# Interleaved rising and falling loads of batch 1, and one angle operation moved, in a fused Fourier mixing and SwiGLU kernel

## The chip, the cores and the metric

The kernel runs on one core of a Trainium2 chip. The metric is the time of one execution in device microseconds (us); smaller is better. The kernel before takes 603.95 us, the median of three runs (603.82 to 604.01). The profile shows one further execution, which took 604.29 us, of which 602.4 us are the span from its first to its last instruction.

The engines are TensorE (PE in the profile, its weight loads PEld), VectorE (DVE), ScalarE (ACT), GpSimd (POOL) and SyncE (SP), which here only issues DMAs (SPq). Each works through a queue of its own in order, and waits on semaphores for the others.

## The reference

```python
def _attn_ref(x):                       # x: (8, 3008, 256)
    X = np.fft.fft(x, axis=1)
    X = np.fft.fft(X, axis=2)
    return X.real
def _moe_ref(x, w_gate, w_val, w_out):  # 24064 tokens, 256 -> 1536 -> 256
    g = x @ w_gate
    silu = g * (1.0 / (1.0 + np.exp(-g)))
    val = x @ w_val
    return silu * val @ w_out
```

Eight batches of 3008 rows and 256 columns are Fourier transformed along both axes; the real part is fed, row by row, to a SwiGLU block with a hidden width of 1536.

## The kernel before, in words

**What it computes.** The column transform is folded into the weights: `Wp`, `Wq` and `Wm` are the gate and value weights multiplied by cosine and sine tables (`half_w`, L458, and `weight_op`, L1794). The row transform of a batch is done by folding its rows by symmetry into few sums, which are multiplied by cosine and sine tables (`Tab`) on TensorE. The results are put by VectorE into the tiles `Pt` (cosine part) and `Qt` (sine part) of 512 columns each (L636 in the start, L1773 later). A unit is one tile and one of the 12 blocks of 128 hidden rows. Part a (L1426) multiplies `Pt` and `Qt` with the weights and gives the values of the rows k; part b (L1482) adds the mirrored sine part and gives those of the rows M - k. VectorE, ScalarE and GpSimd form the products: `hp` (L1550 on VectorE, L1556 on GpSimd) for the rows k and `hm` (L1547 on GpSimd, two blocks at a time) for the mirrored ones. What `hm` reads, `sv`, is written by VectorE (L1539) and ScalarE (L1523) and has two buffers. The first tiles are done whole (L1353): `hp` at L1374 and `hm` at L1395, both on VectorE. TensorE then multiplies with `Wo` (L1598), ScalarE evicts (L1604), SyncE stores (L1610).

**The start.** Batch 0 is loaded, folded and transformed by code in a written order (L251 to L680), all engines at once. The part that the change touches stands from L559 on. GpSimd forms the first rows' coefficients (`heads`, L446), copies a column to `EOA` (L564), and later fills `kfO` with an iota (L674), multiplies it by four columns into `rrO`, rounded to whole turns (`turns`, L352, four operations of 376 columns), and subtracts what will be `BBa` (L678 to L680). VectorE forms the first transform's P puts (L636), waits for ScalarE's copy `od` (L631), forms the Q puts, and casts one half of `Wp` (L468). The angles (`angles`, L356) take the fraction of a turn, `kfO` times a column less the rounded product, one operation for each of two columns and each of two chunks `ch`; magnitude, cosine and sine follow (L362, L368, L365) and fill the table for odd rows, which batch 0's second transform needs (L1756, at 37 us). `kfO` and `rrO` lie in the half of the buffer `XA` that the falling rows of A use; the other half holds the second part of the raw weights.

**The planner.** All later work is added to a list (`S.add`) with an engine, an estimated cost, what it reads and writes, and a due time: TensorE's clock at that point, plus a shift by kind (`SHIFT`) and by tile (`BIAS`). `S.run` (L1174) plays this list with the estimated costs and writes each engine's queue in the order that results. It starts each engine at a given time (L1996). A DMA has two costs, `us` for SyncE's issue and `ring` for the transfer, and no more than eight are under way; in the program itself the DMAs take eight semaphores in turn, so an issue waits until the DMA eight places back has landed. So changed estimates alter no operation, but can change the order on any engine.

**The loads around the change.** Batch 1 is loaded in two parts, while the first tiles are computed: C, 60 rows of partitions (L152), then A, 128 partitions (L146). A part has rising rows, loaded by many small DMAs (C: 15 of 4 partitions, L158; A: 16 of 8 partitions, L148), and falling rows, loaded by few large ones (C: 8, L167, since batch 1 has to lie in partitions 64 to 123 for one half and 0 to 59 for the other; A: 4 of 128 partitions, L150). C of batch 1 also has a load of row 0 (L160) and a copy of its rising rows within the chip (L171), which waits for all 15 rises. All are issued by SyncE: the rises of a part first, then its falls. `run_loads` (L1659) adds four loads for each unit to the planner. Ahead of them SyncE writes zeros to `XC` (L660), and GpSimd's queue loads the second part of the raw weights (L387) and `Wo` (L1970, landed at 36.42 us).

GpSimd folds each part (L173): `cross` (L180 and L181), `even` (L184), `odd` (L187), `ab` (L190), `ce` (L193, L194) and `bb` (L202 to L204). The folds of C and A of batch 1 stand in GpSimd's queue among the `hm` products, in the order that the planner gave.

Of the kernel before, what the change touches and what calls it, by code (L numbers as in the profile page):

```python
# [13 lines left out]
I32 = mybir.dt.int32  # L14
# [17 lines left out]
def kernel(  # L32
# [8 lines left out]
    nc = tc.nc  # L41
# [4 lines left out]
    G = M // 8  # L46
# [19 lines left out]
    NCR = GH - P  # L66
# [64 lines left out]
    LA, NA = 8, P // 8  # L131
# [8 lines left out]
    def down_set(b, a, j, L, n):  # L140

        return rows_at(b, R * (a + 1) - 2 * j, [[2 * L * D, n], [-2 * D, L], [1, 2 * D]])

    JA, JC = P - LA + 1, GH - LC + 1

    def load_a(b, q):  # L146
        X3 = XA.rearrange("p a q d -> p a (q d)")
        return ([lambda h=h: q.dma_start(out=X3[LA * h:LA * (h + 1), 0:4, :],  # L148
                                         in_=up_block(b, JA - LA * h, LA)) for h in range(NA)] +
                [lambda a=a: q.dma_start(out=X3[:, 4 + a, :], in_=down_set(b, a, JA, LA, NA)) for a in range(4)])  # L150

    def load_c(b, q):  # L152

        X3 = XC.rearrange("p a q d -> p a (q d)")
        p0 = 64 * (b % 2)
        pm = p0 + NCR
        r = slice(p0, p0 + NCR)
        ups = [lambda h=h: q.dma_start(out=X3[p0 + LC * h:p0 + LC * (h + 1), 0:4, :],  # L158
                                       in_=up_block(b, JC - LC * h, LC)) for h in range(NC_)]
        mid = [lambda: q.dma_start(out=XC[pm:pm + 1, 0:4, 1],  # L160
                                   in_=rows_at(b, 0, [[R * D, 1], [R * D, 4], [1, D]]))]
        if b != 1:
            return ups + [lambda a=a: q.dma_start(out=X3[r, 4 + a, :], in_=down_set(b, a, JC, LC, NC_))
                          for a in range(4)] + mid

        def down(a, k):
            q.dma_start(out=XC[0:NCR, 4 + a, 0] if k else XC[r, 4 + a, 0],  # L167
                        in_=rows_at(b, R * (a + 1) - 2 * JC + k, [[2 * LC * D, NC_], [-2 * D, LC], [1, D]]))

        downs = [[lambda a=a, k=k: down(a, k) for a in range(4)] for k in range(2)]  # L170
        return ups + downs[0] + mid + [lambda: q.dma_start(out=XC[0:NCR, 0:4, 1], in_=XC[r, 0:4, 0])] + downs[1]  # L171

    def fold_steps(eng, X, CE, BB, q, r):  # L173
        tt = eng.tensor_tensor
# [74 lines left out]
    q = nc.sync  # L249
# [103 lines left out]
        for i in range(2):  # L353
            pts(t1[:, i, :], kf, scalar1=mM[:, 2 * ch + i:2 * ch + i + 1], scalar2=1.0, op0=Alu.mult, op1=Alu.mult)

    def angles(rr, kf, ch, t1):  # L356
        for i in range(2):
            vstt(rr[:, i, :], kf, mM[:, 2 * ch + i:2 * ch + i + 1], t1[:, i, :],
                 op0=Alu.mult, op1=Alu.subtract)

# [85 lines left out]
    def heads(eng, ev, od, CE):  # L446

        eng.tensor_tensor(CE[:, :, 0, 0, -1:], ev, od, op=Alu.add)
        eng.tensor_tensor(CE[:, :, 0, 1, -1:], ev, od, op=Alu.subtract)
# [111 lines left out]
    ptt(hd, SA[:, 0, 0:2, :, 0:1], SA[:, 0, 2:4, :, 0:1], op=Alu.add)  # L561
    heads(nc.gpsimd, hd[:, 0], hd[:, 1], CEa)
    heads(nc.gpsimd, SC[:, 0, 0, :, 0:1], SC[:, 0, 1, :, 0:1], CEc)
    nc.gpsimd.tensor_copy(EOA[:, 0, :, :, P:P + 1], SA[:, 0, :, :, 0:1])  # L564
    ptile, qtile = {}, {}

# [45 lines left out]
    def transform(b, part, eos, given=None):  # L612
        n = NCE if part == 0 else G
        ev, ods = {}, {}
        for q, pool, nm in ((0, psO, "o"), (1, psG, "g")):
            if given:
                ps = {eo: given[eo][q] for eo in eos}
            else:
                ps = {eo: pool.tile([P, T], F32, name=nm) for eo in eos}
                for eo in eos:  # L620
                    mms = products(b, part, q, eo)
                    for i, (l, r_, cols) in enumerate(mms):
                        nc.tensor.matmul(ps[eo][:, cols], l, r_, start=(i == 0), stop=(i == len(mms) - 1),
                                         skip_group_check=True)
            if part == 0 and 1 in eos and not given:

                row0(b, q, ps[1])
            for eo in eos:
                if q == 0:
                    ods[eo] = odp.tile([P, NCE], F32, name="od")  # L630
                    nc.scalar.copy(ods[eo][:, 0:n], ps[eo][:, 0:n])  # L631
                else:
                    ev[eo] = ps[eo]

        def put(eo, dst, s0, w, minus):
            nc.vector.tensor_tensor(dst, ev[eo][:, s0:s0 + w], ods[eo][:, s0:s0 + w],  # L636
                                    op=Alu.subtract if minus else Alu.add)

        if part == 0:
            runs = [(0, GH, 1, 0), (GH, GH, 0, 1), (G, GH, GH + 1, 0), (G + GH, GH, GH + 1, 1)]  # L640
        else:
            runs = [(2 * G, G, 0, 0), (3 * G, G, 0, 1)]
        todo = []
        for eo in eos:
            for c0, n_, s0, minus in runs:
                for t, off, src, w in pieces(b * H + c0, n_):
                    todo.append((t, eo, off, s0 + src, w, minus))
        for t, eo, off, s0, w, minus in sorted(todo, key=lambda v: v[0:2]):
            put(eo, pq_tiles(t)[eo][:, off:off + w], s0, w, minus)
        if part == 0:  # L650
            for eo in eos:
                put(eo, last[eo][:, b:b + 1], 0, 1, 0)
# [8 lines left out]
                    in_=zeros[64 * hi + NCR:64 * hi + 64].unsqueeze(1).to_broadcast([64 - NCR, 16, D]))  # L661
    folded_c(0)
    transform(0, 0, (0,), acc)
    for k in range(2):
        half_w(0, k, psO, "o")
    folded_c(1)
# [4 lines left out]
    for k in range(2):  # L671
        half_w(1, k, psO, "o")
    double(1)
    nc.gpsimd.iota(kfO, pattern=[[4, G]], base=1, **iota)  # L674
    turns(rrO[:, 0].bitcast(I32), kfO, 0)
    turns(rrO[:, 1].bitcast(I32), kfO, 1)
    E_, O_ = EOA[:, 0].rearrange("p a q d -> p q a d"), EOA[:, 1].rearrange("p a q d -> p q a d")
    ptt(BBa[:, :, 0], E_[:, :, 0:4:3, 0:P], E_[:, :, 2:0:-1, 0:P], op=Alu.subtract)  # L678
# [980 lines left out]
    def run_loads(n):  # L1659
        for what, k, fn in loads[:n]:  # L1660
            up = k < (NA if what[0] == "A" else NC_)
            r, w, us, ring = [], [((what[0],), k)], 0.4 if up else 0.62, 0.57 if up or what[0] == "C" else 1.14
            if what == ("A", 1):
                r = [(("C",), NC_ + 9)]
                us, ring = 0.6, 0.6 if up else 0.9
            if what == ("C", 1):
                us, ring = (0.6, 0.6) if k < NC_ else (0.9, 0.9)
                if k == NC_ + 5:
                    r = [(("C",), j) for j in range(NC_)]
            S.add("SP", us, fn, r=r, w=w, after=[(("A",), "pre" if k > 15 else "preW")] if what == ("A", 1) else [],  # L1670
                  lat=2.5, ring=ring)
        del loads[:n]

# [160 lines left out]
    raO = SDf.rearrange("p a d -> p (a d)")[:, 0:4 * G].rearrange("p (c q n) -> p c q n", c=2, q=2)  # L1834

    def angle_op(ch):
        S.add("DVE", 1.1, lambda: angles(rrO[:, ch], kfO, ch, rrO[:, ch].bitcast(I32)),
              r=[(("A",), "pre")], w=[(("rr",), ch)])
        S.add("DVE", 0.7, lambda: magnitude(raO[:, ch], rrO[:, ch]), r=[(("rr",), ch), (("A",), "pre")],
              w=[(("ra",), ch), (("fold",), "F")])  # L1840
# [152 lines left out]
    part_b(prev)  # L1993
    owork = OWork(prev[0], ((psG, "g"), (psV, "v"), (psO, "o")))
    owork.run(len(owork.steps))
    S.run({'DVE': 1.2, 'ACT': 0.9, 'POOL': 3.5, 'PE': 0.0, 'SP': -2.0})  # L1996


# [28 lines left out]
```

## Time and profile before

| what | value |
|---|---|
| median of three runs | 603.95 us |
| the profiled execution | 604.29 us |
| its span | 602.4 us |
| 20 to 45 us: TensorE, VectorE, ScalarE, GpSimd busy | 24.01, 23.09, 23.33, 10.88 us |
| 45 to 64 us | 18.87, 17.74, 17.06, 14.33 us |
| 64 to 100 us | 35.24, 35.44, 32.43, 35.84 us |
| 100 to 150 us | 49.01, 47.72, 45.01, 49.69 us |
| share of the DMA engines busy, 0 to 30 us, in stretches of 10 us | 0.85, 0.99, 0.83 |
| granted clock of TensorE | 1.00 up to 580 us |

A row of a timeline reads: start in us, duration in us, engine, line, operation, tiles written and read, shape, number of like instructions merged; in brackets the idle time of the engine ahead of it and what ended it. A matmul's duration includes its passage through the array, so that rows overlap: the pace is read from one start to the next. The landing of a DMA is not in these rows; it is read from the updates of its semaphore in the trace.

### The profile page before, as it was taken

The numbers are of one execution on the slowest core, as the hardware profiler recorded it, in microseconds if no ns is written. First come the engines' busy times: TensorE is split into PE (matmuls) and PEld (weight loads), VectorE is DVE, ScalarE is ACT, GpSimd is POOL, SyncE is SP. The second block draws the span as 40 slices with busy tenths as digits, with TensorE's granted clock in tenths as the row PEclk, the third lists the DMA queues.
The fourth block names the chain that finished last, engine by engine and source line by source line (L and its number), as shares of the span: only waits on it lengthen the run. The fifth ranks groups of instructions, "written<-read, shape, count | busy, mean of one in ns | idle before, by whom it ended". The sixth has DMA issues, their size and how long they took to land.

```text
span 602.4 us, 12497 instructions
## 1 busy us (share of the span) xinstructions
PE 591.5 (98%) x3974; PEld 392.1 (65%) x4031; DVE 572.8 (95%) x1055; ACT 562.6 (93%) x1086; POOL 509.4 (85%) x460
## 2 busy tenths in 40 slices
PE   9999999999999999999999999999999999999997
PEld 6456666665666666666666666666666666666686
DVE  8989999999999999999999999999999999999993
ACT  8899997999998999999999999999999999999994
POOL 8736999999799999998999988888878467687772
PEclk9999999999999999999999999999999999999999
DMA  9847447254616324464145212036211212111112
GB/s 240 137 98 147 115 117 189 83 132 124 171 40 152 93 66 125 111 140 125 53 91 133 61 53 73 19 100 175 63 62 37 63 38 71 39 53 51 54 53 79
DMA packets 50554, 57.65 MB, mean 96 GB/s; under 512 B 7267, under 2 KB 37399, under 8 KB 50489
## 3 DMA queue, kind: packets, MB, share of 16 engines
q1 hardware_dynamic: 47529, 53.97, 33.4%
q0 software_dynamic: 2672, 2.36, 2.7%
q8 instruction: 31, 0.51, 0.4%
q10 hardware_dynamic: 288, 0.52, 0.3%
q14 instruction: 34, 0.28, 0.2%
HBM read 29.43 MB, written 24.65 MB: 90 GB/s over the span
## 4 chain that ended last, share of the span: by engine, by line
PE 81%; DMA 6%; DVE 4%; ACT 3%; POOL 2%; issue 2%; SPq 2%; POOLq 0%; ACTq 0%; DVEq 0%
PE o L1598 36%; PE g L1336 22%; PE v L1336 18%; PE g L1756 2%; DMA XC<-in_x_dram 2%; PE o L1756 2%; DMA XC<-Af 2%; DVE sv L1539 1%; DMA XA<-in_x_dram 1%; SPq L167 1%; DMA out_dram<-ev 1%; PE v L1598 1%; DVE hp L1550 1%; ACT sp L1448 1%; ACT v L1409 1%
## 5 line engine op out<-in xcount | busy, mean ns | idle before, releaser
L1547 POOL TENSOR_TENSOR hm<-sv 128x1024 bf16<-128x1024 f32 (+2 forms) x137 | 254.9, 1862 | 49.8 <-ACT sv L1523 23.0
L1539 DVE SCALAR_TENSOR_TENSOR sv<-es,v 128x512 f32<-128x512 f32 (+2 forms) x264 | 176.1, 672 | 5.9 <-PE v L1336 4.2
L1598 PE MATMUL o<-Wo,hm 128*128 128x256 bf16 (+1 forms) x1128 | 163.8, 272 | 0.4
L1550 DVE TENSOR_TENSOR hp<-sp,v 128x512 bf16<-128x512 f32 (+2 forms) x238 | 158.1, 672 | 4.4 <-PE v L1336 3.8
L1598 PE MATMUL o<-Wo,hp 128*128 128x256 bf16 (+1 forms) x1104 | 159.7, 272 | 0.7
L1598 PEld LDWEIGHTS <-hm 128*128 128x128 bf16 (+2 forms) x1140 | 111.7, 98 | 58.7 <-issue 2.1
L1598 PEld LDWEIGHTS <-hp 128*128 128x128 bf16 (+2 forms) x1140 | 111.9, 98 | 55.3 <-issue 2.0
L1523 ACT ACTIVATE sv<-g 128x512 f32<-128x512 f32 (+2 forms) x182 | 121.3, 682 | 5.5 <-PE g L1336 4.5
L1448 ACT ACTIVATE sp<-g 128x512 f32<-128x512 f32 (+2 forms) x182 | 113.4, 628 | 4.7 <-PE g L1336 1.9
L1409 ACT ACTIVATE v<-bc,w 128x512 f32<-128x512 bf16 (+2 forms) x146 | 105.9, 727 | 2.9 <-DVE hp L1550 1.6
L1336 PE MATMUL g<-Pt,Wp 128*128 128x512 bf16 (+2 forms) x282 | 105.6, 374 | 1.6 <-ACT sp L1520 0.7
L1336 PE MATMUL v<-Pt,Wp 128*128 128x512 bf16 (+2 forms) x287 | 105.2, 375 | 0.5
L1473 DVE SCALAR_TENSOR_TENSOR es<-bc,w,v 128x512 f32<-128x512 bf16 (+2 forms) x128 | 93.5, 734 | 2.8 <-PE v L1336 0.6
L1471 ACT ACTIVATE es<-v 128x512 f32<-128x512 f32 (+2 forms) x146 | 90.8, 625 | 4.5 <-PE v L1336 2.0
L1336 PE MATMUL g<-Qt,Wq 128*128 128x512 bf16 (+2 forms) x247 | 90.7, 374 | 0.3
L1336 PEld LDWEIGHTS <-Wp 128*128 128x128 bf16 x576 | 56.3, 98 | 26.9 <-issue 1.9
L1336 PE MATMUL g<-Qt,Wm 128*128 128x512 bf16 (+2 forms) x191 | 71.5, 376 | 0.4
L1452 DVE SCALAR_TENSOR_TENSOR sg<-bc,w,g 128x512 f32<-128x512 bf16 (+2 forms) x92 | 66.4, 724 | 1.4 <-PE g L1336 1.0
L1523 ACT ACTIVATE sv<-sg 128x512 f32<-128x512 f32 (+2 forms) x92 | 64.4, 704 | 1.0 <-DVE sg L1516 0.9
L1520 ACT ACTIVATE sp<-g 128x512 f32<-128x512 f32 (+2 forms) x92 | 57.3, 623 | 4.6 <-DVE sg L1516 4.4
L1516 DVE SCALAR_TENSOR_TENSOR sg<-sg,g 128x512 f32<-128x512 f32 (+2 forms) x92 | 60.9, 662 | 0.3 <-PE g L1336 0.2
L1336 PEld LDWEIGHTS <-Wq 128*128 128x128 bf16 x430 | 42.0, 98 | 28.1 <-issue 4.5
(196 smaller groups left out, 772.2 us busy)
## 6 DMA issues: line engine op xcount, KB each, us to landing
out_dram<-ev SPq DMA_DIRECT2D x96, 128.0 KB
XA<-in_x_dram SPq DMA_DIRECT2D x30, 256.0 KB
XA<-in_x_dram SPq DMA_DIRECT2D x112, 64.0 KB
XC<-in_x_dram SPq DMA_DIRECT2D x28, 120.0 KB
XC<-in_x_dram SPq DMA_DIRECT2D x105, 32.0 KB
bc<-br SPq DMA_DIRECT2D x19, 128.0 KB
St<-Fc SPq DMA_DIRECT2D x12, 128.5 KB
out_dram<-ev SPq DMA_DIRECT2D x12, 120.0 KB
```

The lines of the kernel that those rows point to most:

```text
L1336: nc.tensor.matmul(ps[:, :n], Wt[:, gv, fs], src[:, :n], start=start, stop=stop, skip_group_check=True)
L1409: nc.scalar.activation(T_[kv][:, :w], bc[t][:, :w], AF.Copy, scale=w0[:, 1, f:f + 1])
L1448: nc.scalar.activation(sp_to()[:, :w], T_[kg][:, :w], AF.Silu)
L1452: nc.vector.scalar_tensor_tensor(T_[keg][:, :w], bc[t][:, :w], w0[:, 0, f:f + 1], T_[kg][:, :w], op0=Alu.mult, op1=Alu.add)
L1471: nc.scalar.activation(T_[kes][:, :w], T_[kv][:, :w], AF.Copy, scale=2.0 if on_pool(u) > 1 else 1.0)
L1473: nc.vector.scalar_tensor_tensor(T_[kes][:, :w], bc[t][:, :w], w0[:, 1, f:f + 1], T_[kv][:, :w], op0=Alu.mult, op1=Alu.add)
L1516: nc.vector.scalar_tensor_tensor(T_[kgm][:, :w], T_[keg][:, :w], 2.0, T_[kg][:, :w], op0=Alu.mult, op1=Alu.subtract)
L1523: nc.scalar.activation(sv()[:, f % 2, w - 1::-1, 1], T_[kgm if by_dve else kg][:, :w], AF.Silu)
L1539: nc.vector.scalar_tensor_tensor(sv()[:, f % 2, w - 1::-1, 0], T_[kes][:, :w], 2.0, T_[kv][:, :w], op0=Alu.mult, op1=Alu.subtract)
L1547: nc.gpsimd.tensor_tensor(hts_(t)[1][:, f - 1:f + 1, :w], sv()[:, :, :w, 1], sv()[:, :, :w, 0], op=Alu.mult)
L1550: nc.vector.tensor_tensor(hts_(t)[0][:, f, :wp], T_[ksp][:, :wp], T_[kv][:, :wp], op=Alu.mult)
L1598: nc.tensor.matmul(st["ps"][:n, j, :], hts[t][minus][:, f, c:c + n], Wo[:, f, :], start=(f == 0), stop=(f == nF - 1))
```

## The change

Two things are moved, and the planner's estimates for batch 1's loads are set anew.

1. C of batch 1 is issued in the order `C1_ORDER`: u is a rise, d one of the first four falls, e one of the second four, m row 0, c the copy within the chip. A of batch 1 goes by `A1_ORDER`: four rises, one fall, four times.
2. The iota and the first two turns move on GpSimd from behind the start's last doubling to right behind the heads, ahead of the copy to `EOA`. The first of the four angle operations moves on VectorE out of the planner's list into the written start, between the P puts and the Q puts.
3. Estimates: a rise of C 0.35 and 0.45 us (issue and ring) instead of 0.6 and 0.6, a fall of C 0.85 and 0.75 instead of 0.9 and 0.9, a rise of A 0.35 and 0.5 instead of 0.6 and 0.6, a fall of A 0.65 and 0.9 instead of 0.6 and 0.9. A now follows C's last rise in the list instead of C's last fall, and SyncE starts at 1.0 instead of -2.0.

No operation is added or taken away: every engine has the same instructions in both programs, in another order. TensorE's order differs in its matmuls 129 to 249, 516 to 782 and 963 to 1047 of 4025, and in two swaps behind. GpSimd's queue has the first two rows of A's fold (L180, L181) and then: before, `hm`, `even`, `hm`, `odd`, `hm`, `ab`, `hm`; after, `even`, `odd`, `hm`, `hm`, `ab`. On VectorE one `hp` (L1550) and one `sv` (L1539) have changed places there. On SyncE eight C loads of the next batches stand ahead of the first stores.

```diff
+    C1_ORDER = "uuduuduuduuduumuueuueuece"
+    A1_ORDER = "uuuuduuuuduuuuduuuud"
+
     def load_a(b, q):
         X3 = XA.rearrange("p a q d -> p a (q d)")
-        return ([lambda h=h: q.dma_start(out=X3[LA * h:LA * (h + 1), 0:4, :],
+        res = ([lambda h=h: q.dma_start(out=X3[LA * h:LA * (h + 1), 0:4, :],
                                          in_=up_block(b, JA - LA * h, LA)) for h in range(NA)] +
                 [lambda a=a: q.dma_start(out=X3[:, 4 + a, :], in_=down_set(b, a, JA, LA, NA)) for a in range(4)])
+        return in_order(A1_ORDER, u=res[:NA], d=res[NA:]) if b == 1 else res
+
+    def in_order(order, **todo):
+        todo = {k: list(v) for k, v in todo.items()}
+        return [todo[k].pop(0) for k in order]
...
-        return ups + downs[0] + mid + [lambda: q.dma_start(out=XC[0:NCR, 0:4, 1], in_=XC[r, 0:4, 0])] + downs[1]
+        return in_order(C1_ORDER, u=ups, d=downs[0], e=downs[1], m=mid,
+                        c=[lambda: q.dma_start(out=XC[0:NCR, 0:4, 1], in_=XC[r, 0:4, 0])])
...
-    def angles(rr, kf, ch, t1):
-        for i in range(2):
+    def angles(rr, kf, ch, t1, only=(0, 1)):
+        for i in only:
...
     heads(nc.gpsimd, SC[:, 0, 0, :, 0:1], SC[:, 0, 1, :, 0:1], CEc)
+    nc.gpsimd.iota(kfO, pattern=[[4, G]], base=1, **iota)
+    turns(rrO[:, 0].bitcast(I32), kfO, 0)
     nc.gpsimd.tensor_copy(EOA[:, 0, :, :, P:P + 1], SA[:, 0, :, :, 0:1])
...
     transform(0, 0, (0,), acc)
+    angles(rrO[:, 0], kfO, 0, rrO[:, 0].bitcast(I32), (0,))
...
     double(1)
-    nc.gpsimd.iota(kfO, pattern=[[4, G]], base=1, **iota)
-    turns(rrO[:, 0].bitcast(I32), kfO, 0)
     turns(rrO[:, 1].bitcast(I32), kfO, 1)
...
             if what == ("A", 1):
-                r = [(("C",), NC_ + 9)]
-                us, ring = 0.6, 0.6 if up else 0.9
+                r = [(("C",), C1_ORDER.rindex("u"))]
+                us, ring = (0.35, 0.5) if A1_ORDER[k] == "u" else (0.65, 0.9)
             if what == ("C", 1):
-                us, ring = (0.6, 0.6) if k < NC_ else (0.9, 0.9)
-                if k == NC_ + 5:
-                    r = [(("C",), j) for j in range(NC_)]
-            S.add("SP", us, fn, r=r, w=w, after=[(("A",), "pre" if k > 15 else "preW")] if what == ("A", 1) else [],
+                us, ring = (0.35, 0.45) if C1_ORDER[k] == "u" else (0.85, 0.75)
+                if C1_ORDER[k] == "c":
+                    r = [(("C",), j) for j, o in enumerate(C1_ORDER) if o == "u"]
+            S.add("SP", us, fn, r=r, w=w, after=[(("A",), "pre" if A1_ORDER[k] == "d" else "preW")] if what == ("A", 1) else [],
                   lat=2.5, ring=ring)
...
-        S.add("DVE", 1.1, lambda: angles(rrO[:, ch], kfO, ch, rrO[:, ch].bitcast(I32)),
+        S.add("DVE", 1.1 if ch else 0.6, lambda: angles(rrO[:, ch], kfO, ch, rrO[:, ch].bitcast(I32), (0, 1) if ch else (1,)),
               r=[(("A",), "pre")], w=[(("rr",), ch)])
...
-    S.run({'DVE': 1.2, 'ACT': 0.9, 'POOL': 3.5, 'PE': 0.0, 'SP': -2.0})
+    S.run({'DVE': 1.2, 'ACT': 0.9, 'POOL': 3.5, 'PE': 0.0, 'SP': 1.0})
```

## The prediction, made before the changed kernel ran

> **What bounds the kernel now.** I read the page's chain first, then TensorE's timeline row by row, then the rows of the other engines around each hole.
>
> ```profile
> PE 591.5 (98%) x3974; PEld 392.1 (65%) x4031; DVE 572.8 (95%) x1055; ACT 562.6 (93%) x1086; POOL 509.4 (85%) x460
> ...
> PE 81%; DMA 6%; DVE 4%; ACT 3%; POOL 2%; issue 2%; SPq 2%; POOLq 0%; ACTq 0%; DVEq 0%
> ```
>
> TensorE bounds it. The change removes no matmul (4025 in both programs), so it can only close or open holes between matmuls. To find them I took, for each row of TensorE's timeline, the distance to the next start, less the row's own pace (0.204 us for 480 columns, 0.217 for 512, 0.109 for 256). Some 70 holes of 0.21 us are spread evenly over the run: each is one missing matmul record, not a wait. Between 21 and 597 us only three holes over 0.3 us are left, two of them here:
>
> ```profile
> 22.90 0.37 PE L1336 MATMUL g<-Qt,Wq 128*128 128x480 bf16 x1
> 24.02 0.36 PE L1336 MATMUL v<-Qt,Wm 128*128 128x480 bf16 x1 [0.76 <-DVE hp L1374]
> ...
> 63.43 0.60 PE L1598 MATMUL o<-Wo,hm 128*128 128x256 bf16 x4
> 64.57 0.38 PE L1336 MATMUL g<-Pt,Wp 128*128 128x512 bf16 x1 [0.54 <-ACT sv L1523]
> ```
>
> Hole 1: 24.02 - 22.90 - 0.20 = 0.92 us. Hole 2: 64.57 - 63.43 - 0.44 = 0.70. Hole 3, at 141.8 us behind ScalarE: 0.81 + 0.27 = 1.08. All that the change can win is 2.7 us of 604.
>
> **Hole 1, the angle operation.** VectorE's and GpSimd's rows:
>
> ```profile
> 17.09 1.27 DVE L636 TENSOR_TENSOR Pt<-g,od 128x188 bf16<-128x188 f32 x6
> 19.19 1.27 DVE L636 TENSOR_TENSOR Qt<-g,od 128x188 bf16<-128x188 f32 x6 [0.83 <-ACT od L631]
> 20.37 0.68 DVE L468 CAST Wp<-o 128x512 bf16<-128x512 f32 x1
> 20.97 2.44 DVE L358 SCALAR_TENSOR_TENSOR XA<-XA,mM 128x376 f32<-128x376 f32 x2
> 23.33 1.21 DVE L1374 TENSOR_TENSOR hp<-sg,v 128x480 bf16<-128x480 f32 x2
> ...
> 17.97 2.25 POOL L354 TENSOR_SCALAR XA<-XA,mM 128x376 int32<-128x376 f32 x4
> 20.18 1.27 POOL L678 TENSOR_TENSOR BBa<-EOA 128x512 bf16<-128x512 f32 x1
> 21.41 1.58 POOL L679 TENSOR_TENSOR BBa<-EOA 128x512 bf16<-128x512 f32 x1
> ```
>
> The reader is to see 0.83 us in which VectorE waits for the od copy, and two angles behind it that take 2.44 us ahead of the hp product on which hole 1 waits. By the record of line 358 the two took 0.90 and 1.62 us; the shortest angle took 0.60. The change puts the first into the idle 0.83.
>
> Step by step: the heads end at 17.33, the iota (0.44) and the first turn (0.57) end at 18.4, so the angle can start at 18.5. Both slow angles ended 0.42 us behind the end of the GpSimd row that ran beside them (21.45 to 21.87, 22.99 to 23.41); the second turn now runs 18.4 to 19.0, so I let the angle end at 19.4. The Q puts then start 0.2 late, at 19.4, and end at 20.7, while TensorE takes its first Q matmul at 21.25: no loss there. Behind the puts and the cast stands one angle: 21.2, beside the BBa subtraction, to 22.3. Then the Wp cast (0.60 to the next start) and hp, done at 23.5. TensorE's new order puts one matmul of the next unit ahead of the one that waits, so it arrives at 23.3 and waits 0.2. **Gain 0.7 us.** Bounds: 0.92 won (no wait left) to 0.7 lost (both angles take the longest row, 1.62). Next in line is the second weight half, which landed at 24.15; TensorE is there at 24.3. Queued behind the waiting angle on VectorE are only those puts; the moved EOA copy (0.2) is read at 23.07 first, and the turns, already ahead of the BBa subtractions, cost GpSimd nothing new.
>
> The Trainium skill (SBUF — State Buffer, "Who interferes with whom") speaks against this place: a VectorE instruction with two SBUF inputs and a GpSimd instruction that reads SBUF exclude each other, and the later one waits for the other's whole end. The 0.42 above, twice, agrees. Without that rule the angle would end at 19.1 and the gain be 0.9 instead of 0.7.
>
> **Hole 2, the loads.** GpSimd's and SyncE's rows:
>
> ```profile
> 53.70 1.28 POOL L1556 TENSOR_TENSOR hp<-sp,pp 128x512 bf16<-128x512 f32 x1
> 59.49 2.35 POOL L180 TENSOR_TENSOR SDf<-XA 128x1020 f32<-128x1020 f32 x1 [4.51 <-DMA out_dram<-ev]
> 61.97 1.89 POOL L1547 TENSOR_TENSOR hm<-sv 128x1024 bf16<-128x1024 f32 x1
> ...
> 18.15 11.56 SPq L158 DMA_DIRECT2D XC<-in_x_dram  x15
> 32.20 3.61 SPq L167 DMA_DIRECT2D XC<-in_x_dram  x4
> 41.67 8.39 SPq L148 DMA_DIRECT2D XA<-in_x_dram  x16
> ```
>
> GpSimd is idle for 4.5 us until batch 1's last A load has landed (59.20 by the trace's semaphore updates; the release named is a store that shares the count). Its in-order queue holds the hm product behind the first fold step; hm ends at 63.86, ScalarE's sv, which needs its buffer, at 64.52, and TensorE gets its bank at 64.57. So hole 2 moves with that landing.
>
> *C loads.* An issue waits until the DMA eight places back has landed. The seven first rises landed from 26.9 to 29.4, then none until 32.19: the Wo load, 1536 packets of 512 B, holds the DMA engines. Only then come ten slow issues (eight falls at 0.84 to 1.29, one at 0.65, the copy at 0.89), up to 41.5. Interleaved, two falls issue at 19 to 21.6, where SyncE only waits (20.6 to 24.9), and two falls and the row-0 load by 30.6. At 0.35 to 0.5 us a rise, and about 0.35 a fall on the same engines, the last rise lands at 37.6, the copy, which waits for all rises, issues then, one fall behind it, and A starts at 39.6: 2.1 earlier. Bounds: 0 (the copy waits longer) to 4.4 (five slow issues hidden).
>
> *A loads.* Before, 17.5 us from first issue to last landing. Rises land every 0.57 to 0.84, the four falls every 0.94 at the end, and the last four rises are slowed by 1.06 in all by the falls. The nearest row to an interleaved fall is at 95 us: three stores of together 256 KB, a fall's size, between two rises of the next A load. They put these 1.24 apart instead of 0.57, so a fall costs 0.67. Saved: 4 x 0.27 + 1.06 = 2.1; landing at 39.6 + 15.4 = **55.0**. The other bound is nothing saved here, 57.1 (first rival).
>
> The changed GpSimd queue has two more fold steps (1.04, 1.05) ahead of that hm, so hm starts 0.29 + 2.48 + 2.09 = 4.86 behind the landing: at 59.9 instead of 61.97. TensorE is then 0.7 ahead and would like hm 0.7 + 0.6 = 1.3 earlier; it comes 2.1 earlier. **Hole 2 closes: gain 0.6** (of 0.70, with 0.1 left for VectorE's hp, now queued behind the sv that waits for hm). Full closure holds up to a landing at 55.8; from 57.1 on the change loses here.
>
> **The rest.** The planner, whose costs for these DMAs the change also sets, deals the same operations in another order from 20 to 45 us (TensorE's matmuls 129 to 249), 82 to 121 (516 to 782) and 148 to 160 (963 to 1047); behind that the queues agree but for a few swaps. GpSimd is busy 99.6% from 64 to 100 us and VectorE 98%, so cover is thin: a step that stands wrong by one row costs 0.6 (a VectorE row) to 1.9 (an hm). I take 0, since its idle 4.5 us go to the fold, with 1 us either way. Stores on SyncE now stand behind eight C loads of batches 2 and 3; evictions come 3.7 us or more apart with three buffers, so they can wait. **Sum: -0.7 - 0.6 = -1.3.** The profiled execution took 604.29 (span 602.4 and 1.89 around it) and would take 603.0; the median shown lies 0.34 under it, at 603.95: **602.7**.
>
> **Rivals.**
> - *Interleaving doesn't speed A.* A rise alone keeps the DMA share at 0.52, half of the engines, and updates its count nine times where a fall gives sixteen; so the rises' half carries all rises and half of each fall, in any order, and takes the 17.5 us of before. Landing 57.1, hm where it was: hole 1's gain is waited away at hole 2, and VectorE's hp behind sv adds 0.6 less 0.23 of slack: **604.3**. Against: the 0.67 above. The Trainium skill (DMA: Bandwidth & Descriptors, "Why a DMA increments its semaphore by 16 and not by 1") has the rule that a transfer runs on at most as many engines as divide its outermost size, 8 for a rise; counts and share agree.
> - *Slower: the fold stands ahead of hm and the load is late.* If the copy holds SyncE and the landing is only 0.7 earlier, 58.5, hm starts at 63.4, 1.4 late; with hp behind sv, +2.0: **606.0**. It decides from 57.1 on. For it: two fold steps of 2.1 us in front of an hm that was already late.
> - *Hole 1 stays* (angle blocked twice): only hole 2 closes, **603.3**. This is also the case in which that edit doesn't do what it says.
> - *Hole 3 closes too*, since the work ahead of it is dealt anew: 1.08 more, **601.6**. Against: ScalarE's and VectorE's rows wait there for each other, and no load is among them.
>
> **Chances.** Forecast 0.42 (602.2 to 603.2), A not faster 0.20, slower by the fold 0.15, hole 3 too 0.13, hole 1 stays 0.10. 0.2%, about what a measurement of this kernel can tell from no change, is 1.2 us, and the forecast lies on that edge: I count 0.24 of its 0.42 as faster. Faster 0.24 + 0.13 = 0.37; slower 0.15 + 0.03 of the first rival = 0.18; within 0.45. Range 601.4 to 605.2: it reaches the third hole below, and above the first rival with 0.9 for a wrong row; of the fold rival most is left out.
>
> **What would show it.** Hole 1: one L358 row ahead of the Q puts, ending by 19.4, and no wait on hp L1374 over 0.2. C: A's first issue near 39.6. A: the first XA fold at 55.3 instead of 59.49. Hole 2: no wait on hm L1547 near 62. Wrong if a hole of over 0.3 us stands between 60 and 165 us that was not there, or if hm starts after 61.97.

## The result and the profile after

The changed kernel takes 607.66 us (median of six runs, 607.46 to 608.51); the kernel before, on the same chip, 603.88. The ratio is **1.0062, 95% interval 1.0049 to 1.0075**: slower by 3.8 us, where 1.3 less was forecast. The profiled execution took 607.87, of which 606.1 are its span (before 602.4).

The page's first rows and its chain of work that ended last:

```profile
PE 592.5 (98%) x3974; PEld 392.2 (65%) x4031; DVE 571.4 (94%) x1055; ACT 562.8 (93%) x1086; POOL 509.7 (84%) x460
...
PE 88%; DMA 5%; ACT 2%; issue 1%; DVE 1%; POOL 1%; SPq 1%; DVEq 0%; ACTq 0%
```

No engine is busy for more than 1.0 us longer, and the chain holds even more of TensorE than before (88% instead of 81%). Only the places of the holes tell where the time is. Hole 1 is gone. VectorE's, GpSimd's and TensorE's rows of the changed kernel there:

```profile
18.39 0.60 DVE L367 SCALAR_TENSOR_TENSOR XA<-XA,mM 128x376 f32<-128x376 f32 x1
19.30 1.27 DVE L647 TENSOR_TENSOR Qt<-g,od 128x188 bf16<-128x188 f32 x6 [0.31 <-ACT od L642]
...
21.08 0.60 DVE L367 SCALAR_TENSOR_TENSOR XA<-XA,mM 128x376 f32<-128x376 f32 x1
...
18.51 1.48 POOL L363 TENSOR_SCALAR XA<-XA,mM 128x376 int32<-128x376 f32 x2
...
23.04 0.37 PE L1346 MATMUL v<-Pt,Wp 128*128 128x480 bf16 x1
23.24 0.37 PE L1346 MATMUL v<-Qt,Wm 128*128 128x480 bf16 x1
```

The angle (now L367) takes 0.60 us ahead of the Q puts, the second one 0.60 behind the puts and the cast, and the matmul that waited for hp until 24.02 starts at 23.24, one pace behind the one ahead of it. Hole 2, TensorE's timeline:

```profile
62.51 0.60 PE L1608 MATMUL o<-Wo,hm 128*128 128x256 bf16 x4
65.77 0.38 PE L1346 MATMUL g<-Pt,Wp 128*128 128x512 bf16 x1 [2.67 <-ACT sv L1533]
...
67.62 0.63 PE L1346 MATMUL g<-Qt,Wm 128*128 128x512 bf16 x1
68.05 0.63 PE L1346 MATMUL v<-Qt,Wm 128*128 128x512 bf16 x1
...
70.27 0.38 PE L1346 MATMUL g<-Qt,Wm 128*128 128x512 bf16 x1
```

The hole is 65.77 - 62.51 - 0.44 = 2.82 us long instead of 0.70. Behind it a matmul of 512 columns starts every 0.43 us (67.62, 68.05), and from 70.27 on every 0.22 again, as before the hole. GpSimd's and SyncE's rows say why the hole is there:

```profile
58.59 2.35 POOL L189 TENSOR_TENSOR SDf<-XA 128x1020 f32<-128x1020 f32 x1 [4.03 <-DMA XC<-in_x_dram]
...
61.07 1.09 POOL L193 TENSOR_TENSOR EOf<-SDf 128x512 f32<-128x512 f32 x1
62.11 1.09 POOL L196 TENSOR_TENSOR EOf<-SDf 128x512 f32<-128x512 f32 x1
63.16 3.74 POOL L1557 TENSOR_TENSOR hm<-sv 128x1024 bf16<-128x1024 f32 x2
...
70.58 3.75 POOL L1557 TENSOR_TENSOR hm<-sv 128x1024 bf16<-128x1024 f32 x2
...
39.74 1.51 SPq L151 DMA_DIRECT2D XA<-in_x_dram  x4
...
53.16 0.54 SPq L153 DMA_DIRECT2D XA<-in_x_dram  x1
```

A's first issue comes at 39.74 instead of 41.67, but its last load lands at 58.30 (by its semaphore's updates; the DMA named in the bracket shares the count), only 0.9 earlier than before. The even and odd steps (L193, L196) stand in front of the first hm, which starts at 63.16 instead of 61.97, and the whole rest of this part's fold stands in front of the third hm: 70.58 instead of 67.76.

Laid beside the trace of before, matmul by matmul, TensorE is 0.92 us ahead at 61 us, 1.20 behind at 65.8, 2.67 behind at 71, 2.65 at 135 and 3.40 at its last matmul; 0.3 more lies behind that. So the loss is made within ten microseconds.

### The profile page after: what moved, and what is told of

Same layout as the page of the kernel before. It is cut to its first block, busy times and chain, and to the rows that moved or that the text cites. A ratio compares the mean times of both kernels' runs of the same rounds, so it can differ in the third digit from the quotient of the medians.

```text
span 606.1 us, 12508 instructions
## 1 busy us (share of the span) xinstructions
PE 592.5 (98%) x3974; PEld 392.2 (65%) x4031; DVE 571.4 (94%) x1055; ACT 562.8 (93%) x1086; POOL 509.7 (84%) x460
## 4 chain that ended last, share of the span: by engine, by line
PE 88%; DMA 5%; ACT 2%; issue 1%; DVE 1%; POOL 1%; SPq 1%; DVEq 0%; ACTq 0%
PE o L1608 38%; PE g L1346 24%; PE v L1346 19%; DMA XA<-in_x_dram 3%; DMA XC<-in_x_dram 2%; PE g L1766 2%; PE o L1766 2%; PE v L1608 1%; PE o L1814 0%; POOL SDf L189 0%; ACT sp L1458 0%; PE o L605 0%; PE g L605 0%; POOL hm L1557 0%; ACT sv L1533 0%
```

## The experiments

**Theory at the start:** the fold steps ahead of the first hm, with a landing that is only 0.9 earlier, make hole 2 longer, and the slow matmuls behind it add the rest. **Rivals:** the interleaved loads are slower by themselves; the changed order of the other engines costs by itself.

One table for all kernels: A's first issue and last landing, the starts of the first and third hm behind it, how far TensorE is behind (+) or ahead of (-) the profiled execution of before at 61, 76 and 135 us and at its last matmul, and the ratio to the kernel before on the same chip (its median is 603.88 beside the changed kernel and 604.3 to 605.0 beside the others). The ratio on record is not the quotient of the two medians; the two differ by up to 0.0025. The columns ahead of the ratio come from one profiled execution each. x_after_again is the changed kernel once more; the others are told of below.

| kernel | issue, landing | hm 1, hm 3 | 61, 76, 135, end | ratio (95%) |
|---|---|---|---|---|
| before | 41.67, 59.20 | 61.97, 67.76 | 0 | 1 |
| changed | 39.74, 58.30 | 63.16, 70.58 | -0.92, +2.59, +2.65, +3.40 | 1.0062 (1.0049-1.0075) |
| x_after_again | 40.13, 58.56 | 63.41, 70.84 | -0.39, +2.85, +2.91, +3.77 | 1.0068 (1.0047-1.0088) |
| x_angle | 41.42, 60.19 | 62.95, 68.75 | -0.61, +2.17, +2.20, +2.82 | 0.9992 (0.9965-1.0018) |
| x_a_rises_first | 40.08, 57.85 | 62.71, 70.13 | -0.97, +0.98, +2.17, +2.96 | 1.0068 (1.0045-1.0091) |
| x_hm_first | 40.21, 58.25 | 61.02, 70.66 | -0.87, +0.89, +2.70, +3.53 | 1.0036 (1.0018-1.0055) |
| x_fold_first | 41.30, 59.25 | 64.11, 69.03 | -0.02, +2.15, +2.15, +2.26 | 1.0050 (1.0020-1.0079) |
| x_pool_before | 40.92, 59.16 | 61.93, 67.73 | -0.43, +0.19, +4.52, +5.45 | 1.0053 (1.0029-1.0076) |
| x_pool_after | 41.17, 56.84 | 61.70, 69.14 | +0.02, -0.25, +0.45, +0.83 | 1.0045 (1.0016-1.0073) |
| x_rises16 | 39.88, 57.27 | 60.03, 65.83 | -1.08, -1.70, +2.42, +3.71 | 1.0026 (1.0002-1.0051) |
| x_c_old | 40.79, 59.20 | 61.96, 67.75 | -0.96, +0.24, +2.86, +3.61 | 1.0059 (1.0035-1.0084) |
| x_est_true | 40.85, 59.01 | 61.77, 67.56 | -0.54, -0.20, -0.11, +0.80 | 0.9986 (0.9969-1.0004) |
| x_est_true2 | 40.25, 58.19 | 60.96, 66.76 | -0.62, -1.00, -0.90, -0.43 | 0.9979 (0.9961-0.9997) |
| x_est_new | 41.48, 61.24 | 66.10, 73.51 | -0.02, +5.38, +5.56, +6.33 | 1.0093 (1.0070-1.0116) |
| x_est_true_rises | 39.95, 59.80 | 62.56, 68.36 | -0.22, +0.59, +0.70, +1.24 | 1.0026 (1.0008-1.0043) |
| x_true_c_old | 40.57, 57.12 | 59.89, 65.69 | -0.65, -1.77, -1.68, -0.92 | 0.9983 (0.9966-1.0000) |
| x_true_both_old | 40.83, 57.29 | 60.05, 65.84 | -0.40, -1.52, -1.43, -1.02 | 1.0012 (0.9986-1.0039) |

**x_angle: item 2 of the change, without items 1 and 3.**

```diff
-    C1_ORDER = "uuduuduuduuduumuueuueuece"
-    A1_ORDER = "uuuuduuuuduuuuduuuud"
+    C1_ORDER = "u" * 15 + "ddddm" + "ceeee"
+    A1_ORDER = "u" * 16 + "d" * 4
...
-    S.run({'DVE': 1.2, 'ACT': 0.9, 'POOL': 3.5, 'PE': 0.0, 'SP': 1.0})
+    S.run({'DVE': 1.2, 'ACT': 0.9, 'POOL': 3.5, 'PE': 0.0, 'SP': -2.0})
```

(and the estimates of the loads as before)

> The angle operation and the turns alone are moved; orders and estimates of the loads are those of before. Theory (hole 2 is set by the landing of A, whatever TensorE does ahead of it): no wait on hp near 24 us, TensorE 0.9 us ahead up to 62 us, A lands at 59.2 as before, hole 2 grows from 0.70 to 1.6, and the time stays at 603.9 (603.5 to 604.4). Rival (the recorded step: closing hole 1 is worth 0.7 by itself): 603.2.

More differs than the angle and the turns: the estimate of one angle operation (0.6 instead of 1.1) is part of the plan, and with it the planner deals TensorE's matmuls 130 to 208, 235 to 249, 531 to 782 and 964 to 974 in another order than before. Batch 1's loads keep theirs.

603.69 us beside 604.68. Hole 1 is gone and TensorE is 0.6 ahead at 61 us; then it waits at hole 2 for as long as the landing says (60.19 in the profiled execution, not the expected 59.2, and a hole 2 of 2.31 us). The interval holds both the theory's "nothing" and the forecast 0.7; what the trace shows is where the lead ends.

**x_a_rises_first: the changed kernel with A's order of before.**

```diff
-    A1_ORDER = "uuuuduuuuduuuuduuuud"
+    A1_ORDER = "u" * 16 + "d" * 4
```

> The changed kernel with A's 16 rises ahead of its 4 falls again; all engines but SyncE have the same order as in the changed kernel. Theory (the eight DMA engines that carry the rises, and half of every fall, are the bound, so A's order is indifferent): A lands at 58.3, within 0.5, and the time stays at 607.7 (607.0 to 608.3). Rival 1 (interleaving saves the recorded 2.1 us, and something else held A back): landing 60.4, 609.8. Rival 2 (interleaving itself made A slower, 18.6 instead of 17.5 us): landing 57.2, hole 2 of 1.7 us, 605 or, if the clock still falls, 606.5.

609.19 lies above the theory's range, but the landing, 57.85, is within its 0.5, and the ratio is 1.0068, no smaller than the changed kernel's: A's new order doesn't make the loss. The profile also shows that the slow matmuls are not needed for it. Hole 2 is 2.41 us here and the matmuls behind it run at full pace, so TensorE is only 0.98 behind at 76 us; but it loses the rest between 80 and 112 us, with waits for ScalarE of 0.30 at 84.53 and 0.41 at 88.58, and at 135 it is 2.17 behind.

**x_hm_first and x_fold_first: the even and odd steps moved across the hm products, in the changed kernel back, in the kernel before forward.**

```diff
-            queue[what, q][j]()
+            steps = queue[what, q]
+            if what == ("A", 1) and q == 0:
+                for n in {1: (), 2: (), 3: (1, 2, 3)}.get(j, (j,)):
+                    steps[n]()
+            else:
+                steps[j]()
```

(x_hm_first; x_fold_first has `{0: (0, 1, 2), 1: (), 2: ()}` in the kernel before)

> The changed kernel with the even and odd steps of A's first fold moved behind the two hm products on GpSimd; nothing else is moved. Theory (the loss is hm's lateness, 2.09 us of fold steps ahead of it, and the half clock that the long wait brings): A lands at 58.3, hm starts at 61.1 instead of 63.2, hole 2 is about 0.7 instead of 2.82, the granted clock stays at 1.00 from 66 to 70 us, and the time is 607.7 - 2.1 - 1.7 = 603.9. Rival (the loss lies in the other order of the rest of the run): 607 or more. Third case (lateness alone, the clock falls anyway): 605.6.

> The kernel before, in which only the even and odd steps of A's first fold are moved ahead of the first of the three hm products on GpSimd. Theory: A lands at 59.2 as before, hm starts at 64.06 instead of 61.97, hole 2 is 0.70 + 2.09 = 2.8 us, the granted clock falls to 0.5 for about 3.4 us behind it, which costs another 1.7: 603.9 + 2.1 + 1.7 = 607.7. Rival 1 (the clock has nothing to do with the length of the wait): 606.0. Rival 2 (the two steps done early make up for it later): 604 to 605.

x_fold_first has the hm and the hole that the theory said, 64.11 and 2.87 us, and a median of 607.99 (603.84 to 611.40). The clock didn't fall in its profiled execution, which took 606.55, so the 1.7 us for the clock are not shown here, and Rival 1's 606.0 fits that execution as well. **But x_hm_first refutes the theory.** Hole 2 shrinks to 0.63 us and no matmul is slow behind it, but the kernel stays slower than before (ratio 1.0036, median 608.05), and at 135 us TensorE is 2.70 behind, as in the changed kernel. The rows of its timeline with a wait:

```profile
63.63 0.38 PE L1346 MATMUL g<-Pt,Wp 128*128 128x512 bf16 x1 [0.47 <-ACT sv L1533]
73.98 0.38 PE L1346 MATMUL g<-Qt,Wq 128*128 128x512 bf16 x1 [0.81 <-DVE sg L1462]
75.09 0.38 PE L1346 MATMUL g<-Pt,Wp 128*128 128x512 bf16 x1 [0.51 <-ACT sv L1533]
...
85.06 0.38 PE L1346 MATMUL g<-Qt,Wm 128*128 128x512 bf16 x1 [0.73 <-ACT sp L1458]
```

The wait that hole 2 gave up comes back in smaller ones from 73 us on, where VectorE and ScalarE are late. The third hm stands behind the whole fold here as in the changed kernel (70.66), and the fifth is as late (77.87).

**x_pool_before and x_pool_after: GpSimd's queue exchanged as a whole.** Second theory: not one hm, but GpSimd's order over all seven. `A1_FOLD` says which fold steps (part, step) run behind which hm.

```diff
+    A1_FOLD = {1: "01", 2: "02", 3: "03", 4: "05 04", 5: "10", 6: "11 12 13", 7: "14 15"}
+    def fold_after_hm(n):
+        hm_done.append(n)
+        for step in A1_FOLD.pop(n, "").split():
+            queue[("A", 1), int(step[0])][int(step[1])]()
...
             nc.gpsimd.tensor_tensor(hts_(t)[1][:, f - 1:f + 1, :w], sv()[:, :, :w, 1], sv()[:, :, :w, 0], op=Alu.mult)
+            if hm_done:
+                fold_after_hm(len(hm_done))
```

(x_pool_before; x_pool_after has `{0: "01 02", 2: "03 05 04", 4: "10 11", 5: "12 13", 6: "14 15"}` in the kernel before)

> The changed kernel, in which only GpSimd's queue is put back: the steps of both parts of A's fold stand between the same hm products as before (one step behind each of the first three, instead of two steps ahead of the first and three ahead of the third). TensorE, VectorE, ScalarE and SyncE keep the changed order. Theory (fold steps ahead of the first, third and fifth hm are the loss): A lands at 58.3, the first five hm start 0.9 earlier than before (61.0, 63.9, 66.9, 69.8, 74.3), hole 2 is at most 0.8, no half clock, and the time is 603.9 - 0.9 = 603.0 (602.4 to 603.8). Rival (the changed order of the other engines costs by itself): 605 or more.

> The kernel before, in which only GpSimd's queue is put in the changed order (fold steps ahead of the first, third and fifth hm); all other engines and all loads are as before. Theory: A lands at 59.2, the first hm starts at 64.1 and the third at 71.4 instead of 67.8, TensorE is 2.2 us late behind hole 2 and 3 us or more behind the third hm: 603.9 + 3 = 607 (606.3 to 608.5), with or without a fall of the clock, since what the clock loses would have been lost at the third hm. Rival (only the first hm counts): 606.0, and 607.7 where the clock falls.

**The second theory falls too, by half.** x_pool_before takes 608.60 where 603.0 was expected. All hm start as early as before (67.73 the third) and TensorE is nearly level at 76 us. Then TensorE's timeline shows, at 85:

```profile
85.02 0.38 PE L1346 MATMUL g<-Qt,Wm 128*128 128x512 bf16 x1
87.29 0.26 PE L1781 MATMUL g<-Tab,CEa 128*128 128x189 bf16 x1 [1.89 <-POOL CEa L202]
```

TensorE's changed order has batch 1's transform, which needs the whole fold, earlier than GpSimd's old order delivers it. x_pool_after is slower than before (607.84, as expected), but its profiled execution (605.10), with the earliest landing of all (56.84), is only 0.45 behind at 135 us: the changed GpSimd order cost little in the one profile in which A came early.

**x_rises16 and x_c_old: what bounds the loads.** Both stand on x_pool_before; x_c_old adds the old `C1_ORDER` (as in x_angle), x_rises16 this:

```diff
+        if b == 1:
+            ups = [lambda h=h: q.dma_start(out=X3[16 * h:16 * (h + 1), 0:4, :],
+                                           in_=up_block(b, P - 15 - 16 * h, 16)) for h in range(8)]
+            return in_order("uuduuduuduud", u=ups, d=res[NA:])
```

> As x_pool_before, but A of batch 1 is loaded by 8 rises of 16 partitions instead of 16 of 8: the same bytes in packets of the same size, with 16 partitions in the outermost dimension. The rows of every second block of 8 partitions then come in another order than the fold needs, so the output of batch 1 is not the reference's. Theory (a rise runs on half of the DMA engines, and this half is the bound of A): a rise's count now gives 16 updates besides its first, A takes 10 to 12 us instead of 17.5 to 18.8 and lands before 52, hole 2 is gone, and the time is 602.5 (602.0 to 603.3). Rival (the bound is the memory or the packets, not the engines): A lands at 57 to 58.5, and the time is that of x_pool_before.

> As x_pool_before, but C of batch 1 goes in its old order (15 rises, four falls, row 0, the copy, four falls); only SyncE's queue differs from x_pool_before. Theory (interleaving C saves the issue time that the trace shows, 41.7 - 39.7 = 2.0 us at A's first issue, of which 0.9 arrive at A's landing, as A's first loads then wait for the copy): A's first issue at 41.6, landing 59.2, hm 0.9 later than in x_pool_before, time 603.9, which is 0.9 above x_pool_before. Rival (C's order is worth the full 2.0): landing 60.3, 2.0 above x_pool_before.

A rise of x_rises16 gives 16 updates, so it uses all engines, and A still takes 17.4 us (a median of 607.39). The busy table from 42 to 56 us, of x_rises16 first and then of the changed kernel (the last two columns are the DMA engines' share, which adds up the packets' times and so can pass 1, and GB/s):

```profile
42.00:56.00 14.00, 13.96 (x89) 8.79 (x88) 13.63 (x24) 12.36 (x23) 11.38 (x12) 1.00 1.07 139
```

```profile
42.00:56.00 14.00, 13.86 (x87) 8.77 (x88) 13.62 (x23) 12.35 (x23) 11.36 (x12) 1.00 0.71 134
```

At a share of 1.07 instead of 0.71 the rate is 139 GB/s instead of 134: in this stretch a packet of 2 KB takes 247 ns in the mean instead of 170. So the theory of the eight engines falls, and what bounds these reads stays open. Hole 2 is gone in x_rises16 (TensorE 1.70 ahead at 76 us), and the wait for CEa takes it back. x_c_old lands where x_pool_before does (59.20, 59.16) and takes as long (608.15, 608.60), so neither the theory's 0.9 us nor the rival's 2.0 is there.

**x_est_true and x_est_new: only the planner's numbers.** Third theory: all engines' orders were laid out for a landing that doesn't come. On the planner's own clock (its list with the estimated starts and ends, printed) the changed kernel's A lands at 30.35 and its last hm ahead of the fold starts at 29.55; that hm starts at 51.44 in the trace, so the plan expects A at 30.35 + 21.9 = 52.3, and it comes at 58.30. The kernel before planned 36.2 with that hm at 29.85 (51.85 in the trace): 58.2, and it came at 59.20.

```diff
-                us, ring = (0.35, 0.5) if A1_ORDER[k] == "u" else (0.65, 0.9)
+                us, ring = (0.35, 0.8) if A1_ORDER[k] == "u" else (0.65, 1.2)
```

(x_est_true, in the changed kernel)

```diff
-                us, ring = 0.6, 0.6 if up else 0.9
+                us, ring = (0.35, 0.5) if up else (0.65, 0.9)
...
-                us, ring = (0.6, 0.6) if k < NC_ else (0.9, 0.9)
+                us, ring = (0.35, 0.45) if k < NC_ else (0.85, 0.75)
...
-    S.run({'DVE': 1.2, 'ACT': 0.9, 'POOL': 3.5, 'PE': 0.0, 'SP': -2.0})
+    S.run({'DVE': 1.2, 'ACT': 0.9, 'POOL': 3.5, 'PE': 0.0, 'SP': 1.0})
```

(x_est_new, in the kernel before)

> The changed kernel with two numbers of the planner's estimate altered: a rise of A 0.8 us of transfer instead of 0.5, a fall 1.2 instead of 0.9. The planner then puts A's landing where the trace has it (planned 36.35, which is 58.3 on the trace's clock; the changed kernel plans 30.35, which is 52.3). The order of all loads and the moved angle stay as changed. Theory (the loss comes from an order that was planned for a landing 6 us too early: fold steps ahead of hm products on GpSimd and batch 1's transform early on TensorE): A lands at 58.3 still, hole 2 is about 0.7, no wait for CEa, and the time is 0 to 1 us under before, ratio 0.9985 to 1.000. Rival (the loads' order itself, or the moved angle, costs): ratio 1.005 or more, as in x_pool_before.

> The kernel before with nothing altered but the planner's estimates, set to those of the changed kernel (planned landing 31.95 instead of 36.2): same loads in the same order, same angle operations, same instructions. Theory: GpSimd's fold steps come ahead of the hm products as in the changed kernel, A lands at 59 as before, and the time is 2 to 4 us above before, ratio 1.004 to 1.006. Rival (estimates are indifferent, the loads' order made the loss): ratio 1.000.

> The changed kernel once more, beside the others on the same chip. Both theories: ratio 1.005 to 1.0075, landing 58 to 58.6; the half clock behind hole 2 (2.7 us of idle time) comes in some executions and not in others, as it did in the profiles so far, and the time with it by at most 1 us, since the third hm is 2.8 us late anyway.

**This settles it.** Two numbers of an estimate take the changed kernel from ratio 1.0068 to 0.9986 (603.91 us; 608.20 beside it), and the estimates alone, without a load or an angle moved, take the kernel before to 1.0093 (609.38), more than the expected 1.004 to 1.006. In the program x_est_new has the changed kernel's order on TensorE from matmul 250 on, and on GpSimd in all but the four operations that item 2 moves: the estimates alone deal that order. GpSimd's timeline of x_est_true, then TensorE's of x_est_new:

```profile
61.77 1.90 POOL L1557 TENSOR_TENSOR hm<-sv 128x1024 bf16<-128x1024 f32 x1
63.62 1.09 POOL L193 TENSOR_TENSOR EOf<-SDf 128x512 f32<-128x512 f32 x1
64.66 1.90 POOL L1557 TENSOR_TENSOR hm<-sv 128x1024 bf16<-128x1024 f32 x1
```

```profile
63.41 0.60 PE L1598 MATMUL o<-Wo,hm 128*128 128x256 bf16 x4
68.72 0.38 PE L1336 MATMUL g<-Pt,Wp 128*128 128x512 bf16 x1 [4.71 <-ACT sv L1523]
```

In x_est_true hm stands right behind the cross again, although A lands at 59.01. In x_est_new's profiled execution A landed late, at 61.24; the plan had it at 31.95 + 21.7 = 53.7, and hole 2 is 68.72 - 63.41 - 0.44 = 4.87 us. It loses more than the changed kernel (ratio 1.0093 against 1.0068), whose loads landed 2.7 to 2.9 us earlier in its two profiles. The changed kernel's second profile (x_after_again) landed at 58.56 and had the half clock again.

**x_est_true_rises, x_true_c_old, x_true_both_old, x_est_true2: the loads under a plan that fits.** All four have x_est_true's order on every engine but SyncE, with A's order of before, C's, both, and neither.

```diff
-        return in_order(C1_ORDER, u=ups, d=downs[0], e=downs[1], m=mid,
+        return in_order("u" * 15 + "ddddm" + "ceeee", u=ups, d=downs[0], e=downs[1], m=mid,
```

(x_true_c_old; the edit of A's order is that of x_a_rises_first)

> As x_est_true, with A's 16 rises ahead of its 4 falls; only SyncE's queue differs. Theory (A takes 17.5 to 18.8 us in either order): as x_est_true within 0.5 us. Rival (interleaving costs up to 1 us, as the first profiles hint: 18.0 to 18.6 against 15.7 to 18.8): up to 1 us faster.

> As x_est_true, with the loads of C of batch 1 in the order of before; only SyncE's queue differs from x_est_true. Theory (C's order brings A's first issue 1.1 forward, 41.3 to 40.2 in the mean of the profiles so far, but A's first load then waits 0.75 longer, 3.6 instead of 2.9 us from issue to landing): 0.3 above x_est_true. Rival (the whole 1.1 arrives): 1.1 above x_est_true.

> As x_est_true, with all loads of batch 1 in the order of before; only SyncE's queue differs. What is left of the change is the moved angle and a plan that fits the landing. Theory (A's order is worth the 1.7 between x_est_true and x_est_true_rises, C's 0.3): 2.0 above x_est_true, ratio 1.001 to 1.003. Rival (loads' orders are indifferent, and x_est_true_rises was a chance of its runs): within 0.5 of x_est_true.

> x_est_true once more, beside the other two. Both: ratio 0.997 to 1.000; hole 2 between 0.5 and 1.1 us, no half clock between 60 and 165 us.

C's order makes no difference that these runs can tell: 603.42 with the old, 603.73 with the new. A's does: 605.62 (604.54 to 607.76) with rises first against 603.91 (603.04 to 605.06), where neither the theory nor the rival had a loss, and 605.69 (603.12 to 609.98) against 603.42 (603.07 to 605.18), near the 2.0 that was expected. The second pair is the weaker one: five of its twelve runs with rises first took 604.0 us or less. How A's order does it isn't shown. The profiled landings don't say that an interleaved A is faster: A takes 15.7 to 19.9 us in eight profiles with rises first and 16.6 to 18.6 in eight interleaved ones, with medians of 17.9 and 18.2. What is missing among the interleaved ones is the late landings.

x_est_true (0.9986), x_est_true2 (0.9979) and x_true_c_old (0.9983) have medians about 4 us under the changed kernel's and 0.8 to 1.1 under that of before. Only the interval of x_est_true2 (0.9961 to 0.9997) lies wholly under 1, so the gain over before is barely told. Hole 2 was 0.33 us in x_est_true2's profile, less than the expected 0.5 to 1.1.

## Why the prediction was wrong

1. **Hole 1 (gain 0.7): the edit worked, the gain isn't kept.** The angle ran from 18.39 to 18.99 (forecast 18.5 to 19.4), no wait on hp was left, and TensorE was 0.92 us ahead at 61 us. That the Q puts began at 19.30, as forecast (19.4), is luck: they waited for ScalarE's od, not for the angle. The angle was not blocked. The turn that started beside it at 18.51 was: it took 0.93 us instead of 0.57 to 0.58 and ended 0.45 behind the angle. The Trainium skill (SBUF — State Buffer, "Who interferes with whom") says that the later of two such instructions waits for the other's end; the trace agrees, with GpSimd as the one that waits. In x_after_again, the same program, it was the other way round, as forecast: the turn started at 18.37, ahead of the angle at 18.43, the angle took 0.92 us, and TensorE was 0.39 ahead at 61 us. The lead then ends at hole 2, which a landing sets.
2. **C loads (A's first issue at 39.6): right**, 39.74. Not counted was that A's first load then takes 3.63 us to land instead of 2.86, as the copy and the last falls are still under way: 0.77 of the 1.93 is given back, and under a plan that fits C's order is worth nothing that these runs can tell.
3. **A loads (15.4 us, at most 17.5): the first step that failed.** A took 18.56 us and landed at 58.30 instead of 55.0, so hole 2 did not close, it grew to 2.82 us. The 0.67 for a fall, taken from three stores at 95 us, didn't hold here: the four falls landed 1.28, 1.15, 0.93 and 0.64 us behind the load ahead of them. The first rival was nearer (no gain, 17.5), with the wrong reason: in x_rises16 no half of the engines is the bound, and A takes 17.4.
4. **hm 4.86 behind the landing: exact**, 63.16 - 58.30 = 4.86; with the old order it is 2.77 in every kernel. The fold rival, which I gave 0.15, assumed a landing at 58.5 and hm at 63.4. Its 606.0 lacks the slow matmuls (1.5) and the third hm.
5. **"The rest: I take 0" is the second step that failed, and the one whose repair takes the loss away.** I read the new order for its one hm and gave everything else 1 us either way. But the order is one plan, made from the estimates that the change also sets, and they bring A's landing forward by 5.85 us, where my own loads brought it forward by 4.2 (59.2 to 55.0). Even on my numbers the plan came 2.7 us too early (55.0 against 52.3); it came 6.0 too early on the chip. The price stands in hm 3 (70.58 against 67.76) and in the transform's place on TensorE, and x_est_new shows that it is the estimates'. Whether this order would have cost nothing with loads that land at 55.0 stays open: no run had such loads. A smaller part of this step, 0.75 us between 135 us and the last matmul, is there in x_est_true (0.91) and x_est_true2 (0.47) as well, so the early plan alone isn't its cause, which stays open.
6. **Sum (-1.3): x_est_true comes near it, by luck.** With all loads and the angle moved as changed and a plan that fits, it came out 1.1 and, once more, 0.8 us under the median of before beside it. The terms are not those of the forecast: A landed at 59.01 and 58.19, hole 2 was 1.06 and 0.33 us, and the angle under the same plan without the new loads (x_true_both_old, 605.69 beside 604.50) shows no gain.

## What to carry to other kernels

Where an order is planned from estimates, a change of the estimates is a change of every queue: compare the time that the plan expects with the time that the trace shows, and price the difference on each engine, before counting what the moved instructions themselves save. Here plans whose landing lay within about 1 us of the real one (before, x_est_true) held, and plans that were early by 6.0 (changed) and 7.5 us (x_est_new) lost 3.2 to 4.4 us in the median, as the queues, which run in order, held ready hm products behind fold steps that could not start. Where a hole shrinks and the time doesn't, look for the wait further on (here the third product and the next transform): x_hm_first had its first two products earlier and kept most of the loss.

## What the runs showed of the hardware

**The granted clock falls in stretches of 3.41 us, and a stretch that is half idle is enough.** The changed kernel's table by stretches (PE busy first, the granted clock PEclk third from the end), then that of x_fold_first, whose hole is as long:

```profile
63.08:66.49 3.41, 0.68 (x4) 0.26 (x3) 1.41 (x3) 1.26 (x3) 3.41 (x3) 1.00 0.49 138
66.50:69.91 3.41, 3.41 (x13) 2.28 (x13) 3.01 (x5) 3.17 (x6) 3.33 (x6) 0.50 0.44 136
69.91:73.32 3.41, 3.41 (x26) 2.31 (x25) 3.16 (x6) 2.85 (x7) 3.41 (x4) 1.00 0.33 81
```

```profile
61.83:65.24 3.41, 2.12 (x14) 1.26 (x13) 1.01 (x2) 1.31 (x3) 3.41 (x5) 1.00 0.41 122
65.24:68.65 3.41, 1.93 (x12) 1.21 (x12) 2.50 (x4) 2.46 (x5) 2.62 (x2) 1.00 0.42 112
```

In the changed kernel TensorE is idle for 2.66 us within one stretch, and the next one, 3.41 us long, runs at half the clock: 13 matmul records instead of 26, a loss of 1.5 us. In x_fold_first 2.72 us of idle time lie across two stretches (1.24 and 1.48), and the clock holds. The changes of the clock in a profile lie whole multiples of 3.413 us apart (in the changed kernel at 5.06, 66.50 and 69.91), and this grid lies elsewhere in every execution, so the same hole costs 1.5 us more in one than in another. Waits within one stretch of 1.88 (x_rises16), 1.89 (x_pool_before, 2.23 with smaller ones), 2.15 (x_angle), 2.40 (x_after_again), 2.66 (changed) and 3.03 us (x_est_new) brought the fall; 1.23 and 1.50 (x_c_old), 1.36 (x_est_true_rises), 1.68 (x_est_new) and 1.69 (x_a_rises_first, 1.75 with a smaller one) didn't. The Trainium skill (TensorE: Matmul & The Clock Gate, "Part 1: The HAM clock gate") tells of a free-running window of 3413 ns, which the trace shows; that a whole idle window is needed, as it says, is not so here: these profiles put the limit between 1.69 and 1.88 us, about half of a stretch.

Most of the half clock's loss is not added to the others: x_a_rises_first kept its clock, and at 135 us it was 2.17 behind against the changed kernel's 2.65. It waited at 84.5 and 88.6 us instead, behind hm products that are as late as the changed kernel's (the third at 70.13 against 70.58).

**The same loads take 15.7 to 19.8 us in the same order.** Before, x_fold_first, x_pool_after and x_est_new have the same operations in the same order on SyncE up to the last of A's loads, and A took 17.52, 17.95, 15.67 and 19.76 us. One profiled landing is therefore no measure of an order of loads; it took pairs of kernels with one queue exchanged, and their times, to tell.
